# The global queries' values of a banded attention block: ten products on all 128 rows, ahead of the local values, in place of eighteen on 64 rows behind them

## The chip, the cores and the metric

The kernel runs on one core of a Trainium2 chip. The metric is the device time of one execution in microseconds, the median of three runs. The core has a matrix engine (TensorE, "PE" in the profile, its weight loads listed apart as "PEld"), three engines for elementwise work (VectorE "DVE", ScalarE "ACT", GpSimd "POOL") and a queue from which transfers are issued (SyncE, "SP").

## The reference, cut to what matters

```python
B, H, Sl, D, Sg = 8, 8, 512, 64, 32           # batch, heads, local and global tokens
k_all = concat([k_g, k_l]); v_all = concat([v_g, v_l])
out_g = softmax(q_g @ k_all.T / 8) @ v_all     # 32 global queries look at all 544 keys
mask  = abs(i - j) <= 32                       # 512 local queries: 32 global keys, and a band
out_l = softmax([q_l @ k_g.T, band(q_l @ k_l.T)] / 8) @ concat([v_g, v_l])
x = concat([out_g, out_l])                     # 8 x 544 tokens of 512
a, b = x @ w1, x @ w2                          # 512 -> 1024
out = (a * b) @ w3 @ w_out                     # 1024 -> 1024 -> 512
```

All of it is float32. The change touches one term: `softmax(...) @ v_all` of the 32 global queries.

## The kernel before, in words

The program runs over 32 pairs of heads (8 batches, 4 pairs in each). A pair's scores, softmax and values give 544 tokens by 128 columns of `x`; four pairs complete a batch, whose tokens then pass through the two layers of the feed-forward part. The orders in which the engines get their work are written out as a list (`PLAN`), which stays as it is. In the list the feed-forward products of one batch stand between the attention steps of the next, so that TensorE always has something queued.

The product `w3 @ w_out` is folded once at the start, and all weights are unpacked and split in two parts there, by DVE, ACT and POOL, as they arrive; this is the stage up to about 112 us. The feed-forward products are 128 x 128 (`first`: lines L539 to L541; `second`: L571 to L573).

The attention products work on parts of the 128 x 128 array. A product is placed by the 64 rows that its operands lie on and by the columns that its result goes to, so four products of 64 x 64 lie side by side: (x, y) with x the head of the pair (the half of the columns) and y the half of the rows, called lanes in the code. The scores (L377) use eight places of 64 x 32. Each of these float32 products appears in the trace as two load and product instructions.

`values(m)` computes one pair's values, in the PSUM tile `av` of two banks, one for each y:

- L431: the local queries' band, 16 products (4 blocks of 128 keys, 4 lanes). Their moving operand `PT` is assembled by up to eight small copies, by ACT, DVE, POOL or a DMA (`move`, L418 and L420).
- L436: the 32 global queries over the local keys, 16 products of 32 columns. The moving operand `TG[x]` (tile `TGr`) holds their turned probabilities, 128 keys by 4 blocks, and is fetched once per batch and head parity by five DMAs (L510, L511).
- L440: the local queries over the global keys, 8 products.
- L442: the global queries over the global keys, 2 products on the 64 lower rows. Their moving operand `TGg[x]` has 64 partitions, the upper 32 of them zero.

With y = 0 the global queries' result goes to columns 0 to 31 of bank 0, with y = 1 to columns 480 to 511 of bank 1; `values_odd` copies bank 1 out, `values_ends` the first 64 columns of bank 0, `values_sum` adds the rest, and `join_g` (POOL) adds the two partial results of the global queries.

From the sixth pair of scores on, `values_scores` issues the values of one pair and directly behind them the scores of the next.

Of the kernel before, what the change touches and what calls it, by code (L numbers as in the profile page):

```python
# [7 lines left out]
F32 = mybir.dt.float32  # L8
# [210 lines left out]
def band_attention_glu_kernel(  # L219
# [20 lines left out]
    nc = tc.nc  # L240
# [5 lines left out]
    TG = 32 * B  # L246
    S = 544

    const = ctx.enter_context(tc.tile_pool(name="const", bufs=1))
# [18 lines left out]
    TT = const.tile([128, 4, 2, 4, 32], F32, tag="TT", name="TT")  # L268
# [1 line left out]
    PT = const.tile([128, 4, 2, 4, 32], F32, tag="PT", name="PT")  # L270

    VG = [const.tile([128, 2, H, 64], F32, tag="VG0", name="VG0"), None]
    TGg = [const.tile([64, 128], F32, tag=f"TGg{x}", name=f"TGg{x}") for x in range(2)]
    xg = const.tile([128, NP, TG], F32, tag="xg", name="xg")
    sums = p1q.tile([128, 6, 2, 4], F32, tag="sums", name="sums")[:, 0:2]

# [18 lines left out]
    T = {}  # L295
# [59 lines left out]
    def hi_of(dst, src, eng=None):  # L355
        (nc.scalar.copy if eng in (None, nc.scalar) else eng.tensor_copy)(dst, src)  # L356
# [65 lines left out]
    def values(m):  # L422
        b, p = divmod(m, NP)
        av = T["av", m] = ps_1.tile([128, 2, 512], F32, tag="pu", name=f"av{m}", bufs=2)
        V, vg = T["vr", m], VG[b % 2]
        lanes = [(x, y, slice(64 * x, 64 * x + 64), slice(64 * y, 64 * y + 64)) for x in range(2) for y in range(2)]
        go = dict(skip_group_check=True)
        for k in range(4):
            for x, y, c, r in lanes:
                s0, s1 = int(k == y == 0), 4 - int(k == 3 and y)  # L430
                nc.tensor.matmul(av[c, y, 128 * k + 32 * s0 : 128 * k + 32 * s1], V[r, x, k], PT[r, s0:s1, x, k],  # L431
                                 start=(k == 0), stop=False, **go)
        for k in range(4):
            for x, y, c, r in lanes:
                o = 480 * y
                nc.tensor.matmul(av[c, y, o : o + 32], V[r, x, k], T["TG", x][r, p, 32 * k : 32 * k + 32], start=False, stop=False, **go)  # L436
        for a in range(2):
            for x, y, c, r in lanes:
                o = av[c, y].rearrange("p (e c) -> p e c", e=4)[:, :, 32 + 32 * a : 64 + 32 * a]
                nc.tensor.matmul(o, vg[r, a, 2 * p + x], TT[r, 2 - a, x], start=False, stop=bool(a and y), **go)  # L440
        for x in range(2):
            nc.tensor.matmul(av[64 * x : 64 * x + 64, 0, 0:32], vg[0:64, 0, 2 * p + x], TGg[x][:, 32 * p : 32 * p + 32], start=False, stop=True, **go)  # L442

    def values_scores(m):
        values(m - 1)
        scores(m)

    def values_odd(m, eng):
        u = T["u", m] = p2.tile([128, 576], F32, tag="u", name=f"u{m}")
        hi_of(u[:, 64:576], T["av", m][:, 1], eng)  # L450

    def values_ends(m, eng):
        hi_of(T["u", m][:, 0:64], T["av", m][:, 0, 0:64], eng)
# [5 lines left out]
    def join_g(m):  # L459
        b, p = divmod(m, NP)  # L460
        u = T["u", m]
        nc.gpsimd.tensor_add(xg[:, p, 32 * b : 32 * b + 32], u[:, 0:32], u[:, 544:576])  # L462


    def g_scores(b):
# [303 lines left out]
    def head(m):  # L769
# [44 lines left out]
        if me[0] == "av":  # L814
            add(me, only("PE", COST["values"]), t + 4.2, values_need(m), values, m)
            values_read(m)
        take("u", 2, ("u", m), ("cb", m))
        a, d = COST["cb"]
        add(("cb", m), dict(ACT=(a, False, 0), DVE=(d, False, HOLD_H)), t + 4.7, [me], values_odd, m, eng=True)
        a, d = COST["cu"]  # L820
        add(("cu", m), dict(ACT=(a, False, 0), DVE=(d, False, HOLD_H)), t + 4.8, [me, ("cb", m)], values_ends, m, eng=True)
# [4 lines left out]
    def pair(m):  # L826
        b, p = divmod(m, NP)
        t = base(2 * m + 1)
        add(("joing", m), only("POOL", COST["joing"], True), t + 9.0, [("cb", m), ("cu", m)], join_g, m)
        for e in range(2):  # L830
            x = ("x", b, p, e)
            take(f"x{e}", NX[e], x, ("xh", b, p, e))
            add(("xh", b, p, e), only("ACT", COST["xh"]), t + 9.2 + 0.4 * e, [("sum", m)], convert, b, p, e, 0)
            add(("xl", b, p, e), either("xl"), t + 9.6 + 0.4 * e, [("xh", b, p, e)], convert, b, p, e, 1, eng=True)
            read(("xl", b, p, e), x)
            read(("xh", b, p, e), ("u", m))
            read(("xl", b, p, e), ("u", m))
        read(("joing", m), ("u", m))
# [186 lines left out]
    with tc.manual_schedule(engines=None):  # L1025
        idle_products(IDLE[None])
        for _, n, e in list_schedule(steps, after, held):
            fn, args, eng = emit[n]
            k = steps[n][0]
# [65 lines left out]
```

## Time and profile before

| what | value |
|---|---|
| median of three runs | 754.91 us (754.11 to 755.97) |
| the profiled execution: its own time | 755.88 us |
| its span in the profile | 754.1 us |
| TensorE busy | 742.1 us (98%) |
| TensorE weight loads busy | 650.6 us (86%) |
| VectorE, ScalarE, GpSimd busy | 58%, 43%, 11% |

The span is the stretch from the first to the last instruction; the execution's own time has 1.8 us around it. "Busy" means that at least one instruction of the engine was under way, which for a matrix engine that overlaps its instructions says nothing yet on how fast it goes.

### The profile page before, as it was taken

The page shows a single profiled execution, that of the slowest core. Times are in us where ns is not written, and L with a number is a line of the kernel's source. Part 1 is how long each engine was busy: PE and PEld are TensorE (multiplying, and loading weights), DVE is VectorE, ACT ScalarE, POOL GpSimd, SP SyncE. Part 2 cuts the span into 40 slices and gives each one's busy share as a digit, 9 for nine tenths or more (in the row PEclk, how much of TensorE's full clock was granted, in tenths as well). Part 3 has the DMA queues.
Part 4 walks back from the last instruction along what each step waited for, and adds up shares of the span by engine and source line. Part 5 has one row for each costly group of instructions (what it writes and reads, how often), then busy time and mean ns, then how long its engine had stood idle before and what let it go on. Part 6 is the DMA issues. An engine that isn't in the chain of part 4 may idle for free.

```text
span 754.1 us, 22008 instructions
## 1 busy us (share of the span) xinstructions
PE 742.1 (98%) x9232; PEld 650.6 (86%) x9232; DVE 438.8 (58%) x1332; ACT 326.6 (43%) x989; POOL 84.3 (11%) x153
## 2 busy tenths in 40 slices
PE   9999899999999999999999999999999999999998
PEld 5445689989999999889998999899989999999997
DVE  4989997674756455573558465665566464312121
ACT  3649876633544244443435334344454343321111
POOL 4013332232100000000001011000000010000000
PEclk9999999999999999999999999999999999999999
DMA  9878565123422211142112411231113010000000
GB/s 333 269 242 313 176 200 160 47 61 118 132 60 87 99 46 59 52 134 73 31 59 87 128 45 43 90 111 31 60 34 120 16 44 4 32 1 30 1 29 28
DMA packets 46171, 69.47 MB, mean 92 GB/s; under 512 B 7768, under 2 KB 22136, under 8 KB 46072
## 3 DMA queue, kind: packets, MB, share of 16 engines
q1 hardware_dynamic: 46072, 68.07, 28.0%
q8 instruction: 72, 1.18, 0.7%
q14 instruction: 27, 0.22, 0.1%
HBM read 53.74 MB, written 13.37 MB: 89 GB/s over the span
## 4 chain that ended last, share of the span: by engine, by line
PE 81%; DVE 7%; DMA 5%; ACT 3%; issue 1%; SPq 1%; DVEq 0%; ACTq 0%
PE bp L539 8%; PE ap L539 8%; PE acc L573 8%; PE acc L571 8%; PE acc L572 8%; PE ap L540 8%; PE ap L541 8%; PE bp L540 8%; PE bp L541 8%; PE s L377 4%; PE av L431 4%; DMA raw_w<-in_w_t_dram 3%; PE av L440 2%; PE av L436 2%; DMA raw_wo<-in_wo_t_dram 1%
## 5 line engine op out<-in xcount | busy, mean ns | idle before, releaser
L539 PE MATMUL bp<-x,w12h 128*128 128x256 f32 x544 | 153.0, 281 | 0.2 <-DVE g__1210 L549 0.2
L539 PE MATMUL ap<-x,w12h 128*128 128x256 f32 x544 | 152.4, 280 | 0.2 <-ACT x L356 0.2
L540 PE MATMUL ap<-x,w12h 128*128 128x256 f32 x544 | 151.1, 278 | 1.0 <-DVE x L359 1.0
L541 PE MATMUL ap<-x,w12l 128*128 128x256 f32 x544 | 150.8, 277 | 0.0
L540 PE MATMUL bp<-x,w12h 128*128 128x256 f32 x544 | 150.7, 277 | 0.0
L541 PE MATMUL bp<-x,w12l 128*128 128x256 f32 x544 | 150.6, 277 | 0.0
L388 ACT ACTIVATE P<-P,small 128x128 f32<-128x128 f32 x256 | 101.0, 396 | 30.8 <-DVE small L382 30.4
L539 PEld LDWEIGHTS bp<-x,w12h 128*128 128x128 f32 x544 | 102.1, 188 | 5.7 <-issue 3.2
L382 DVE CUSTOM_DVE_ANT_0 P<-s,cs 128x128 f32<-128x128 f32 x256 | 64.2, 284 | 71.7 <-PE s L377 70.0
L539 PEld LDWEIGHTS ap<-x,w12h 128*128 128x128 f32 x544 | 102.2, 188 | 3.6 <-issue 1.4
L540 PEld LDWEIGHTS ap<-x,w12h 128*128 128x128 f32 x544 | 102.4, 188 | 3.0 <-DVE x L359 1.3
L540 PEld LDWEIGHTS bp<-x,w12h 128*128 128x128 f32 x544 | 102.3, 188 | 1.5
L541 PEld LDWEIGHTS ap<-x,w12l 128*128 128x128 f32 x544 | 102.3, 188 | 0.0
L541 PEld LDWEIGHTS bp<-x,w12l 128*128 128x128 f32 x544 | 102.3, 188 | 0.0
L356 ACT COPY u<-av 128x512 f32<-128x512 f32 (+1 forms) x58 | 23.6, 412 | 69.0 <-PE av L442 69.0
L420 ACT COPY PT<-TT 32x256 f32<-32x256 f32 (+1 forms) x99 | 38.6, 390 | 29.9 <-DVE PT L406 14.3
L388 ACT ACTIVATION_READ_ACCUMULATOR P<-P,small 128x1 f32 x256 | 48.0, 188 | 0.0
L684 PE MATMUL w<-wo,w3f 128*128 128x512 f32 x96 | 43.4, 600 | 1.8 <-DVE w3f L597 1.2
L403 DVE STREAM_TRANSPOSE TT<-P 128x1024 f32<-128x1024 f32 x32 | 39.5, 1235 | 0.6
L398 DVE TENSOR_TENSOR P<-P,sums 128x1024 f32<-128x1024 f32 x32 | 39.1, 1222 | 0.6
L431 PEld LDWEIGHTS av<-PT,vr 64*64 64x64 f32 x1024 | 28.1, 132 | 13.0 <-issue 8.4
L462 POOL TENSOR_TENSOR xg<-u 128x32 f32<-128x32 f32 x32 | 8.7, 272 | 267.7 <-ACT u L356 233.4
(771 smaller groups left out, 1340.6 us busy)
## 6 DMA issues: line engine op xcount, KB each, us to landing
raw_w<-in_w_t_dram SPq DMA_DIRECT2D x22, 512.0 KB, 6.1
kq<-in_kp_t_dram SPq DMA_DIRECT2D x32, 272.0 KB, 3.5
out_dram<-o_None SPq DMA_DIRECT2D x33, 256.0 KB, 2.3
qp<-in_q_t_dram SPq DMA_DIRECT2D x32, 256.0 KB, 2.7
vr<-in_v_t_dram SPq DMA_DIRECT2D x32, 256.0 KB, 3.1
gg<-tgs SPq DMA_DIRECT2D x16, 272.0 KB, 2.2
raw_wo<-in_wo_t_dram SPq DMA_DIRECT2D x8, 512.0 KB, 9.3
raw_w3j<-in_w_t_dram SPq DMA_DIRECT2D x8, 512.0 KB, 8.3
```

The source lines that it names most:

```text
L382: nc.vector.tensor_tensor_reduce(Ps[m % 2][:, x, e], T["s", m][:, x, 128 * e : 128 * e + 128], masks[e], -0.125, 3.0e38, ALU.add, ALU.min, ...
L388: nc.scalar.activation(p, p, AF.Exp, bias=T["mn", n][:, e : e + 1], scale=-1.0, accum_out=T["sm", m][:, x, e : e + 1])
L398: eng.tensor_mul(p, p, view(T.pop(("sm", m)), 0, [1, 8], [0, 128]))
L403: nc.vector.transpose(view(TT[:], 0, [32, 8], [256, 4], [1, 32]), view(P, 0, [128, 8], [32, 4], [1, 32]))
L431: nc.tensor.matmul(av[c, y, 128 * k + 32 * s0 : 128 * k + 32 * s1], V[r, x, k], PT[r, s0:s1, x, k], start=(k == 0), stop=False, **go)
L539: nc.tensor.matmul(d, wh[:, k, c, :], x[:, 0, 0:w], start=(k == m % 2 == 0), stop=False, skip_group_check=True)
L540: nc.tensor.matmul(d, wh[:, k, c, :], x[:, 1, 0:w], start=False, stop=False, skip_group_check=True)
L541: nc.tensor.matmul(d, wl[:, k, c, :], x[:, 0, 0:w], start=False, stop=(k == 3), skip_group_check=True)
L571: nc.tensor.matmul(a, gh[:, m % 2, sl], wh[:, c], start=(m == 0), stop=False, **part)
L572: nc.tensor.matmul(a, gh[:, m % 2, sl], wl[:, c], start=False, stop=False, **part)
L573: nc.tensor.matmul(a, gl[:, m % 2, sl], wh[:, c], start=False, stop=(m in (5, 7)), **part)
L684: nc.tensor.matmul(T["w34", t], w3f_of(t, j), wo_of(j), start=(j == 0), stop=(j == 7))
```

## The change

The sixteen products of the global queries over the local keys used half the rows each and were summed in two banks. They become eight that use all 128 rows (one for each block of keys and head), and the two products over the global keys use all 128 rows too: `TGg` grows to 128 partitions, and its rows 32 to 127 are zeroed. The ten stand in front of the local values instead of behind them. Everything goes to bank 0, so `values_odd` copies 480 columns instead of 512, and `join_g` copies where it added. The lines behind the edit have numbers lower by one (L431 becomes L436, L440 becomes L441); the new products are L432.

```diff
-    TGg = [const.tile([64, 128], F32, tag=f"TGg{x}", name=f"TGg{x}") for x in range(2)]
+    TGg = [const.tile([128, 128], F32, tag=f"TGg{x}", name=f"TGg{x}") for x in range(2)]
...
         go = dict(skip_group_check=True)
+
+        for k in range(5):
+            for x in range(2):
+                w, t = (V[:, x, k], T["TG", x][:, p, 32 * k : 32 * k + 32]) if k < 4 else (vg[:, 0, 2 * p + x], TGg[x][:, 32 * p : 32 * p + 32])
+                nc.tensor.matmul(av[64 * x : 64 * x + 64, 0, 0:32], w, t, start=(k == 0), stop=False, **go)
         for k in range(4):
             for x, y, c, r in lanes:
                 s0, s1 = int(k == y == 0), 4 - int(k == 3 and y)
                 nc.tensor.matmul(av[c, y, 128 * k + 32 * s0 : 128 * k + 32 * s1], V[r, x, k], PT[r, s0:s1, x, k],
-                                 start=(k == 0), stop=False, **go)
-        for k in range(4):
-            for x, y, c, r in lanes:
-                o = 480 * y
-                nc.tensor.matmul(av[c, y, o : o + 32], V[r, x, k], T["TG", x][r, p, 32 * k : 32 * k + 32], start=False, stop=False, **go)
+                                 start=(k == 0 and y == 1), stop=False, **go)
         for a in range(2):
             for x, y, c, r in lanes:
                 o = av[c, y].rearrange("p (e c) -> p e c", e=4)[:, :, 32 + 32 * a : 64 + 32 * a]
-                nc.tensor.matmul(o, vg[r, a, 2 * p + x], TT[r, 2 - a, x], start=False, stop=bool(a and y), **go)
-        for x in range(2):
-            nc.tensor.matmul(av[64 * x : 64 * x + 64, 0, 0:32], vg[0:64, 0, 2 * p + x], TGg[x][:, 32 * p : 32 * p + 32], start=False, stop=True, **go)
+                nc.tensor.matmul(o, vg[r, a, 2 * p + x], TT[r, 2 - a, x], start=False, stop=bool(a), **go)
...
-        hi_of(u[:, 64:576], T["av", m][:, 1], eng)
+        hi_of(u[:, 64:544], T["av", m][:, 1, 0:480], eng)
...
-        nc.gpsimd.tensor_add(xg[:, p, 32 * b : 32 * b + 32], u[:, 0:32], u[:, 544:576])
+        nc.gpsimd.tensor_copy(xg[:, p, 32 * b : 32 * b + 32], u[:, 0:32])
```

What stands on TensorE at one pair (the fifteenth), before, from the last feed-forward product to the first global queries' products. A row gives line, result, operands and the result's shape; "x10" are ten such in a row, and in brackets stand the engines and DMA queues that a row waits for.

```order
L573 MATMUL acc_1_128_4222<-w34h_483,gl__4180 128x512
L431 MATMUL av_4233<-PT,vr_3760 64x96 [waits DMAHW4_49,Pool_49]
L431 MATMUL av_4233<-PT,vr_3760 64x128 [waits DMAHW1_49]
L431 MATMUL av_4233<-PT,vr_3760 64x96
L431 MATMUL av_4233<-PT,vr_3760 64x128 x10
L431 MATMUL av_4233<-PT,vr_3760 64x96
L431 MATMUL av_4233<-PT,vr_3760 64x128
L431 MATMUL av_4233<-PT,vr_3760 64x96
L436 MATMUL av_4233<-TGr_3428,vr_3760 64x32 x2
L436 MATMUL av_4233<-TGr_3470,vr_3760 64x32 x2
```

The same place of the changed program.

```order
L572 MATMUL acc_1_128_4110<-w34h_483,gl__4068 128x512
L432 MATMUL av_4121<-TGr_3332,vr_3656 64x32 [waits DMAHW4_49]
L432 MATMUL av_4121<-TGr_3374,vr_3656 64x32
L432 MATMUL av_4121<-TGr_3332,vr_3656 64x32
L432 MATMUL av_4121<-TGr_3374,vr_3656 64x32
...
L432 MATMUL av_4121<-TGg_98,VG_1139 64x32
L432 MATMUL av_4121<-TGg_99,VG_1139 64x32
L436 MATMUL av_4121<-PT,vr_3656 64x96 [waits Pool_49]
L436 MATMUL av_4121<-PT,vr_3656 64x128 [waits DMAHW1_49]
```

The ten products come first, one head after the other, and the waits for `PT`'s copies (Pool, and the second DMA queue) moved behind them; one wait for a DMA queue stays on the first. Before, the end of the same pair's values, up to the next pair's scores:

```order
L436 MATMUL av_4233<-TGr_3470,vr_3760 64x32 x2
L440 MATMUL av_4233<-TT,VG_1171 64x4x32 x8
L442 MATMUL av_4233<-TGg_98,VG_1171 64x32
L442 MATMUL av_4233<-TGg_99,VG_1171 64x32
L377 MATMUL s_4276<-KT_92,qp_3513 32x128 x32
```

And in the changed program:

```order
L436 MATMUL av_4121<-PT,vr_3656 64x96
L441 MATMUL av_4121<-TT,VG_1139 64x4x32 x8
L377 MATMUL s_4156<-KT_92,qp_3417 32x128 x32
```

The products on 64 rows are now one block, and the scores stand directly behind the local queries' products over the global keys. On the other engines the order is unchanged.

## Rows read from the trace of the kernel before

**Rows 1.** The profile's page: span, TensorE's busy time, granted clock in 40 slices.

```profile
span 754.1 us, 22008 instructions
PE 742.1 (98%) x9232; PEld 650.6 (86%) x9232; DVE 438.8 (58%) x1332; ACT 326.6 (43%) x989; POOL 84.3 (11%) x153
...
PEclk9999999999999999999999999999999999999999
```

**Rows 2.** Stages, busy us (instructions) per engine: PE, PEld, DVE, ACT, POOL.

```profile
45.00:115.00 70.00, 65.16 (x930) 45.57 (x932) 64.38 (x161) 53.49 (x143) 21.52 (x24) 1.00 0.68 228
115.00:650.00 535.00, 534.18 (x7342) 489.34 (x7324) 320.44 (x1039) 229.77 (x749) 52.69 (x95) 1.00 0.23 72
```

**Rows 3.** The same stages, PE and PEld, instructions of L442 alone.

```profile
45.00:115.00 70.00, 1.55 (x20) 1.53 (x20) 1.00 0.68 228
115.00:650.00 535.00, 7.09 (x108) 6.95 (x108) 1.00 0.23 72
```

**Rows 4.** Timeline of TensorE's products around the fifteenth pair: start, us until the last's end.

```profile
304.92 0.39 PE L572 MATMUL acc<-w34l,gh__4174 128*128 128x512 f32 x1
305.15 0.40 PE L573 MATMUL acc<-w34h,gl__4180 128*128 128x512 f32 x1
305.48 1.05 PE L431 MATMUL av<-PT,vr 64*64 64x96 f32 x32
306.35 0.62 PE L436 MATMUL av<-TGr,vr 64*64 64x32 f32 x32
306.79 0.65 PE L440 MATMUL av<-TT,VG 64*64 64x128 f32 x16
307.25 0.26 PE L442 MATMUL av<-TGg,VG 64*64 64x32 f32 x4
307.44 1.16 PE L377 MATMUL s<-KT,qp 64*32 64x128 f32 x64
308.53 0.39 PE L539 MATMUL bp<-x,w12h 128*128 128x256 f32 x1
308.75 0.28 PE L540 MATMUL bp<-x,w12h 128*128 128x256 f32 x1
```

**Rows 5.** Timeline of its weight loads in the same stretch.

```profile
304.93 0.19 PEld L573 LDWEIGHTS acc<-w34h,gl__4180 128*128 128x128 f32 x1
305.48 0.86 PEld L431 LDWEIGHTS av<-PT,vr 64*64 64x64 f32 x32 [0.36 <-issue]
306.24 0.61 PEld L436 LDWEIGHTS av<-TGr,vr 64*64 64x64 f32 x32
307.44 0.89 PEld L377 LDWEIGHTS s<-KT,qp 64*32 64x32 f32 x64
308.76 0.19 PEld L541 LDWEIGHTS bp<-x,w12l 128*128 128x128 f32 x1
```

**Rows 6.** Products by tile and line: ns of one, minimum/median/maximum; first and last start.

```profile
L431 PE MATMUL av<-PT,vr x1024: 242/269/321, 47.4 to 648.3; 64*64 64x128 f32 x116, 64*64 64x96 f32 x55
L436 PE MATMUL av<-TGr,vr x1024: 189/219/219, 48.3 to 648.8; 64*64 64x32 f32 x171
L440 PE MATMUL av<-TT,VG x512: 269/269/299, 48.7 to 649.2; 64*64 64x128 f32 x171
L442 PE MATMUL av<-TGg,VG x128: 189/204/219, 49.2 to 649.3; 64*64 64x32 f32 x128
...
L377 PE MATMUL s<-KT,qp x2048: 266/269/294, 9.0 to 633.7; 64*32 64x128 f32 x187
```

**Rows 7.** Weight loads of the sixteenth pair, in brackets the idle time before.

```profile
319.71 0.40 PEld L431 LDWEIGHTS av<-PT,vr 64*64 64x64 f32 x8 [0.36 <-issue]
320.47 0.64 PEld L431 LDWEIGHTS av<-PT,vr 64*64 64x64 f32 x24 [0.36 <-DMA PT<-TT]
```

**Rows 8.** Products around the fifth pair.

```profile
111.02 0.28 PE L541 MATMUL ap<-x,w12l 128*128 128x256 f32 x1
112.11 1.11 PE L431 MATMUL av<-PT,vr 64*64 64x96 f32 x30 [0.82 <-ACT PT L420]
```

**Rows 9.** Fetches of `TGg`, 100 to 115 us: issues, and their time to landing.

```profile
L511 SPq DMA_DIRECT2D TGg<-gg x2: 430/430/430, 105.2 to 108.8; - x2
...
DMA to landing us min/median/max: 3.1/3.1/3.1
```

## The prediction, made before the changed kernel ran

> **What bounds the kernel now.** I read the page's head first: TensorE is busy for 742.1 of 754.1 us, every other engine for 58% or less, and its granted clock stands at full speed (2.4 GHz) in all 40 slices [rows 1]. A busy matrix engine need not be a full one, so the stages come next. From 115 to 650 us TensorE is busy for 534.18 of 535 us [rows 2]: 0.8 us of idle time in all, while DVE has 320 us and ACT 230. Here nothing waits but the others, and whatever a pair of heads adds to TensorE's row moves the end by as much. From 45 to 115 us TensorE is busy 65.16 of 70 us and DVE 64.38 [rows 2]; it idles for unpacked weights there, and a small addition can vanish in that. The two products of L442, four instructions a pair, count the pairs: 20 instructions, five pairs, in the early stage, and 108, twenty-seven pairs, in the steady one [rows 3].
>
> So the question is what one pair's values take on TensorE, and the timeline of one pair answers it [rows 4]. From the first load of L431 at 305.48 to the scores at 307.44 it takes 1.96 us: L431 0.87, L436 0.44, L440 0.46, L442 0.19. The reader should see that these are differences of starts; the lengths behind the starts overlap.
>
> **What sets the pace inside.** L436 has 32 instructions (two to a float32 product) on four places that work side by side: eight rounds. From the first start to the last end is 0.62 us, one instruction is recorded with 0.219 [rows 4, 6], so 0.40 us for seven rounds: 57 ns a round. Streaming 32 columns cannot need that: a 128-column instruction takes 80 ns longer than the shortest 32-column one (269 against 189 ns, [rows 6]), 0.83 ns a column, which makes 27 ns for 32. What takes 57 is the weight load. The first product after a change of shape shows its length, since it must wait for a load that nothing hides: L431's longest is 52 ns over its median (321 against 269), with 64 columns of weights; L377's is 25 over (294 against 269), with 32; L539's first is 110 over the product behind it (0.39 against 0.28 us), with 128 [rows 4, 6]. The load goes by the columns of one place, 0.8 to 0.9 ns each, with one place at work (L539), four (L431) or eight (L377) alike. L442 runs on two places only, and its longest is the same 219 ns as L436's [rows 6]: fewer neighbours did not make its second load faster.
>
> **What the change does to a pair.** Removed: L436, eight rounds, and L442, two rounds on half the places. Added: twenty instructions on two places (128 rows, 64 columns each), that is ten rounds. The instructions fall from 36 to 20, the rounds stay at ten. That is the heart of my forecast: rows were not the limit, loads in a row at one place were, and there are as many as before.
>
> *Saved.* L436: 0.44 us, and 0.03 more since L440's first round (longest 299 against a median of 269, [rows 6]) no longer waits for a load behind L436's. L442: not the 0.19 between its start and L377's. A change of shape starts when the last product is nearly out of the array: L442's last ends at 307.51 and L377's load stands at 307.44, 0.07 earlier [rows 4, 5]. Without L442, L440's block ends at 306.79 + 0.65 = 307.44, so L377 may start at 307.37 instead of 307.44. That is 0.07 to 0.08. Together 0.55 us.
>
> *Added.* Ten rounds of 57 ns: 0.57 us. No row shows a place of 128 rows by 64 columns; the bounds are 30 ns a round (27 of streaming and a little issue, if the load were hidden) and 114 (if the two places had to load in turn). I take 57, since two places gave it in L442. Then a new change of shape, 128 rows to 64, ahead of L431. The one in front of the pair stays. Its price in the row: L573 to L431's load is 0.33 us where two L57x products in a row are 0.23 apart (304.92 and 305.15), so 0.10 us with nothing streaming [rows 4], and then a first load of 0.05 us that nothing hides. Sum 0.15; the bounds are 0, if this kind of change needs no emptying, and 0.20 as from L377 to L539: L377's block ends at 308.60, so its last product (0.269) started at 308.33 and streamed 128 columns to 308.44; L539 stands at 308.53, 0.09 later, and its load takes 0.11. I take 0.15, the change of the same place in the program: "[0.36 <-issue]" in front of L431's loads [rows 5] is that gap, and the loads, which otherwise run ahead, do not cross it. In the Trainium skill, "TensorEngine Tiling (Array Packing)", section "Key Properties", a change of tiling mode drains the engine; that speaks against this change. By it the pair pays the 0.15; without it, 0. The trace agrees for the changes that it holds, but none of them keeps the column places and alters the rows alone, as the new one does.
>
> *Net of one pair:* 0.57 + 0.15 - 0.55 = +0.17 us.
>
> *What moves with it.* The waits for `PT`'s copies now stand behind 0.7 us of work. That helps where TensorE waited for them: the sixteenth pair loses 0.56 us in mid-block for a DMA into `PT` [rows 7]; with L431 starting 0.72 later, at 320.43, the copy that arrived at 320.47 is there, so the pair gains about 0.55 - 0.17 = 0.4. The fifth pair stands idle from 111.3 to 112.11 for a copy [rows 8], but its `TGg` was issued at 108.85 and lands 3.1 us later, at 111.95 [rows 9], and is now wanted early: gain and loss cancel, 0. The other 26 steady pairs show 1.96 us without a wait. The first four lie in the stage where TensorE idles 4.8 us for weights; I count them 0, with -0.8 (one wait of the fifth's size, 0.82, hidden) to +0.7 (four times 0.17, nothing absorbed) as bounds. ACT's copy is 32 columns shorter, POOL copies instead of adding, the zeroed tile has more partitions and no more columns: all beside TensorE, which is released by none of them in the steady stage, so 0; if the cover were gone, a copy of `u` would be worth some tens of ns a pair, in the change's favour.
>
> *Sum.* 26 x 0.17 - 0.4 = +4.0 us. The profiled execution took 755.88 us by its own count (span 754.1 and 1.8 around it), so 759.9 on that; the median of the runs is 1.0 lower, 754.91, and what is predicted is a median: **758.9 us**, 0.5% slower.
>
> **The rivals.**
> *The load is hidden and the pair gets faster.* If 57 ns comes from the number of instructions at work rather than from the load, half as many run at the streaming pace of 30 ns: 0.30 + 0.15 - 0.55 = -0.10 a pair, -3.0 in all, 751.9 us. It decides from 40 ns a round downwards. Against it stands L442's 219 ns on two places, and the loads' equal price for one, four and eight. Chance 0.07.
> *No emptying for rows alone.* The column places stay the same, so L431's loads might run ahead as L440's do. Then 0.57 - 0.55 = +0.02 a pair, and with the hidden waits 0 in all: 755 us, no change. For it: no row shows this change of shape. Against it: every change of shape that there is pays. Chance 0.14.
> *The two heads take turns.* The new products alternate head by head and share all rows. If the second instruction of one product had to leave before the other head's first, each of five steps costs a further slot of some 15 ns: +0.07 a pair, +5.8 in all, 760.7 us. Chance 0.08. If the places could not load side by side at all, ten rounds cost 1.14: +0.74, 774 us. Chance 0.03.
> *Loads wait for products on the same rows.* By this a round is 57 + 30 = 87 ns: 0.87 + 0.15 - 0.55 = +0.47 a pair, 26 of them less 0.4: +11.8, 766.7 us. Against it: L541's load starts at 308.76, 0.01 after L540's product started on the same 128 rows [rows 4, 5]. Chance 0.04. This is what the Trainium skill states in "TensorE: Matmul & The Clock Gate", "Part 3: Packing small matmuls" (loads overlap products in flight only on other row groups); the trace disagrees where the whole array is used.
>
> **How the numbers follow.** The forecast has the remaining 0.64; its own range, with the switch at 0.12 to 0.18, a round at 55 to 59 ns and the first four pairs' bounds, is 757 to 761. The range that leaves out no more than 2 in 10 reaches down to the case without emptying and up to the heads in turn: **754.5 to 761.5 us**, 0.86 by the chances, less where I mistook a price. About 0.3%, 2.3 us, is what a measurement here can tell from no change. Slower by more: the forecast (nearly all of it), the turns and both costly cases, 0.76. Within: the case without emptying and a tail of the forecast, 0.16. Faster: the hidden load, 0.08 with a tail.
>
> **What would show it.** In the changed profile the ten products' block should take 0.57 us from its first start to the last and its loads some 57 ns apart at one place; L436 (the local band) should start 0.72 us after the block, behind an idle gap of its own, with its longest products again 52 ns over the median; L441 should follow without its first round's stall, and the scores' first load stand 0.07 us before the end of L441's last product. From the last feed-forward product to the scores a pair should be 0.17 longer. Rounds at 30 ns, or a band whose loads run ahead into the new block, make me wrong; so does a steady stage with idle time on TensorE, which would mean that some wait moved in front of the ten products.

## The result, and the profile after

| | before | after |
|---|---|---|
| median of four runs, taken side by side | 755.2 us (754.11 to 755.97) | 759.3 us (758.74 to 760.38) |
| ratio after/before | | 1.0057, 95% interval 1.0039 to 1.0075 |
| the profiled execution: its own time, span | 755.88 us, 754.1 us | 758.86 us, 757.0 us |

The changed kernel is slower by 0.6%. The forecast was 758.9 us. The page's head answers [rows 1]:

```profile
span 757.0 us, 20984 instructions
PE 746.4 (99%) x8720; PEld 649.6 (86%) x8720; DVE 439.6 (58%) x1332; ACT 325.3 (43%) x989; POOL 83.1 (11%) x153
```

TensorE has 512 product instructions fewer (256 products) and is busy for 4.3 us longer. The other engines hardly moved. Where the time went is seen in one pair. The timeline of products around the fifteenth pair answers [rows 4]; the second fence is the timeline of its weight loads [rows 5].

```profile
306.39 0.40 PE L572 MATMUL acc<-w34h,gl__4068 128*128 128x512 f32 x1
306.72 0.66 PE L432 MATMUL av<-TGr,vr 128*64 128x32 f32 x16
307.20 0.29 PE L432 MATMUL av<-TGg,VG 128*64 128x32 f32 x4
307.42 1.05 PE L436 MATMUL av<-PT,vr 64*64 64x96 f32 x32
308.29 0.62 PE L441 MATMUL av<-TT,VG 64*64 64x128 f32 x16
308.84 1.16 PE L377 MATMUL s<-KT,qp 64*32 64x128 f32 x64
```

```profile
306.72 0.55 PEld L432 LDWEIGHTS av<-TGr,vr 128*64 128x64 f32 x16 [0.36 <-issue]
307.18 0.20 PEld L432 LDWEIGHTS av<-TGg,VG 128*64 128x64 f32 x4
307.42 0.86 PEld L436 LDWEIGHTS av<-PT,vr 64*64 64x64 f32 x32
308.19 0.48 PEld L441 LDWEIGHTS av<-TT,VG 64*64 64x64 f32 x16
308.84 0.89 PEld L377 LDWEIGHTS s<-KT,qp 64*32 64x32 f32 x64 [0.17 <-issue]
```

From the first product to the scores the pair takes 306.72 to 308.84, 2.12 us, where it took 1.96. The ten products, up to the band, are 0.70 of it (forecast 0.72). What is left, from the band to the scores, is 1.42; it was 1.96 with L436 and L442 in it, so leaving these two out saved 0.54 (forecast 0.55). The loads show the two kinds of seam. From L436 to L441, one shape, the first load stands 0.10 us ahead of its product (308.19 and 308.29); but L436's first load, 307.42, stands at the same place as its first product. It did not run ahead across the change from 128 rows to 64; it stands 0.07 us before the end of the last L432 product (307.20 + 0.29 = 307.49), as the scores' first load before the change stood 0.07 us before the end of L442 [rows 4].

The lengths of single products answer [rows 6] (ns, minimum/median/maximum):

```profile
L436 PE MATMUL av<-PT,vr x1024: 242/269/320, 49.4 to 651.8; 64*64 64x128 f32 x117, 64*64 64x96 f32 x54
L432 PE MATMUL av<-TGr,vr x512: 222/223/243, 48.7 to 650.7; 128*64 128x32 f32 x171
L441 PE MATMUL av<-TT,VG x512: 269/269/269, 50.3 to 652.2; 64*64 64x128 f32 x171
```

The band's longest product is still 51 ns over its median: its first load is not hidden. L441's longest is equal to its median: the stall of L440's first round (299 ns) is gone, as forecast.

The sixteenth pair, which had waited for a DMA [rows 7], answers with these loads:

```profile
321.11 0.55 PEld L432 LDWEIGHTS av<-TGr,vr 128*64 128x64 f32 x16 [0.36 <-PE acc L571]
...
321.81 0.86 PEld L436 LDWEIGHTS av<-PT,vr 64*64 64x64 f32 x32
```

Its scores stand at 323.23: 2.12 us, like every other pair; before, they stood at 322.27, 2.56 us after 319.71. So this pair gained 0.44.

The first five pairs did not go as the forecast had them. The fifth had waited for a copy and started at 112.11 [rows 8]; now it starts at 110.83, 1.28 us earlier, and waits neither for `PT` nor for `TGg`. Then its scores' loads stop for 1.15 us, with no wait shown, and that takes the gain back:

```profile
110.83 0.55 PEld L432 LDWEIGHTS av<-TGr,vr 128*64 128x64 f32 x16
...
112.95 0.86 PEld L377 LDWEIGHTS s<-KT,qp 64*32 64x32 f32 x60 [0.17 <-issue]
114.96 0.14 PEld L377 LDWEIGHTS s<-KT,qp 64*32 64x32 f32 x4 [1.15 <-issue]
```

The sixth pair starts at 127.83, before at 127.80. In the ten profiled executions of this document the fifth pair starts anywhere from 109.87 to 113.64, so two of them do not tell what the early stage does with an addition.

The forecast left one wait out. Behind the sixteenth pair TensorE waits once in the whole steady stage for DVE, for the low part `gl` of the feed-forward's inner product. The chain of waits from 328 to 340 us, first before, then after:

```profile
PE acc L573 <- DVE gl__4688 L359: 0.7, 1, 0.7
```

```profile
PE acc L572 <- DVE gl__4560 L359: 0.4, 1, 0.4
```

The later TensorE arrives there, the less it waits: 0.3 us came back. In the profiled executions the sum is thus +4.0 for the 26 steady pairs (25 of them took 0.157 or 0.158 us more, the tenth 0.106; the rows round to 0.16), less 0.44, less 0.3: +3.3, and measured are 758.86 - 755.88 = +3.0. The rest stands in feed-forward products that the change does not touch. Before, from 199 to 206 us and from 339 to 349 us, those of 256 columns followed each other at 0.118 us; in the same places of the changed program they do at 0.113. Ten such steps take 1.18 us before (344.89 to 346.07) and 1.14 after (345.39 to 346.53), with a granted clock of 1.00 in both; the two stretches give 0.2 and 0.3 us, a little more than the rest, and steps of some 0.01 us between other pairs go the other way. Why the pace differs is not shown. The medians differ by 4.1, and their interval (2.9 to 5.7 us) holds both sums.

### The profile page after: what moved, and what is told of

The parts are those of the page before. It is cut to its first block, busy times and chain, and to the rows that moved or that the text cites. A ratio compares the mean times of both kernels' runs of the same rounds, so it can differ in the third digit from the quotient of the medians.

```text
span 757.0 us, 20984 instructions
## 1 busy us (share of the span) xinstructions
PE 746.4 (99%) x8720; PEld 649.6 (86%) x8720; DVE 439.6 (58%) x1332; ACT 325.3 (43%) x989; POOL 83.1 (11%) x153
## 4 chain that ended last, share of the span: by engine, by line
PE 88%; DVE 6%; ACT 3%; issue 2%; DMA 1%; SPq 0%; DVEq 0%; ACTq 0%
PE bp L538 8%; PE acc L572 8%; PE ap L538 8%; PE acc L570 8%; PE acc L571 8%; PE ap L539 8%; PE bp L540 8%; PE bp L539 8%; PE ap L540 8%; PE s L377 4%; PE av L436 3%; PE w L683 3%; PE av L432 3%; PE av L441 2%; ACT P L388 1%
## 5 line engine op out<-in xcount | busy, mean ns | idle before, releaser
L356 ACT COPY u<-av 128x480 f32<-128x480 f32 (+1 forms) x58 | 22.7, 397 | 73.7 <-PE av L441 73.7
L683 PEld LDWEIGHTS w<-wo,w3f 128*128 128x128 f32 x96 | 17.6, 189 | 24.8 <-issue 18.0
L377 PE MATMUL s<-KT,qp 64*32 64x128 f32 x2048 | 37.1, 274 | 0.9 <-issue 0.9
```

The costliest lines, as they stand in the source:

```text
L377: nc.tensor.matmul(st[32 * a : 32 * a + 32, x, 128 * e : 128 * e + 128], q[r, 128 * e + 32 * a : 128 * e + 32 * a + 32], k[r, o : o + 128] ...
L683: nc.tensor.matmul(T["w34", t], w3f_of(t, j), wo_of(j), start=(j == 0), stop=(j == 7))
```

## The experiments

Theory: (a) a round of weight loads of 64 columns at one place takes 57 ns, whatever the rows and however many places; so ten rounds for ten save nothing; (b) the new change of shape costs about 0.15 us a pair and is the whole loss. Rivals: the place in front of the band costs; the streaming or the number of instructions sets the round; the wide rows themselves are slow. In the diffs "-" is the kernel named as the base. Every measured time stands against the kernel before, run beside it.

**The place alone.** Base: the kernel before. The sixteen 64-row products move in front of the band, nothing else.

```diff
         for k in range(4):
             for x, y, c, r in lanes:
+                o = 480 * y
+                nc.tensor.matmul(av[c, y, o : o + 32], V[r, x, k], T["TG", x][r, p, 32 * k : 32 * k + 32], start=(k == 0), stop=False, **go)
+        for k in range(4):
+            for x, y, c, r in lanes:
                 s0, s1 = int(k == y == 0), 4 - int(k == 3 and y)
                 nc.tensor.matmul(av[c, y, 128 * k + 32 * s0 : 128 * k + 32 * s1], V[r, x, k], PT[r, s0:s1, x, k],
-                                 start=(k == 0), stop=False, **go)
-        for k in range(4):
-            for x, y, c, r in lanes:
-                o = 480 * y
-                nc.tensor.matmul(av[c, y, o : o + 32], V[r, x, k], T["TG", x][r, p, 32 * k : 32 * k + 32], start=False, stop=False, **go)
+                                 start=False, stop=False, **go)
```

> The kernel before with one edit: L436's sixteen products of 64 x 64 stand in front of the local values; L442's two stay at the end. Theory 1 (a pair pays 58 ns a round of 64-column weight loads and 0.15 us for the extra change of shape): no extra change of shape, rounds as before, so a steady pair takes 1.96 to 2.00 us from its first product to the scores, and the waits for PT hide as they do in the changed kernel: 753.5 to 755, that is 4 to 6 us under the changed kernel. Rival (the place in front is what costs, whatever the shape): the pair takes 2.12 us and the time is about 759.

Measured: 755.98 us against 755.02; ratio 1.001 (0.9996 to 1.0024). Its timeline of products, fifteenth pair:

```profile
306.70 0.67 PE L431 MATMUL av<-TGr,vr 64*64 64x32 f32 x32
307.19 1.03 PE L435 MATMUL av<-PT,vr 64*64 64x96 f32 x32
...
308.48 0.26 PE L442 MATMUL av<-TGg,VG 64*64 64x32 f32 x4
308.67 1.16 PE L377 MATMUL s<-KT,qp 64*32 64x128 f32 x64
```

306.70 to 308.67 is 1.97: the place costs a pair nothing. The gain that I expected from the hidden wait is in the trace (the sixteenth pair takes 320.94 to 323.02, 2.08) and not in the median. In this execution the sixth pair began at 128.88, where before it was 127.80: from 92.12 to 95.32 us the feed-forward products follow each other at 0.21 to 0.22 us instead of 0.11 to 0.12, since the clock had fallen. The windows of 2.5 us (TensorE's busy time and its granted clock), of this kernel and then of before:

```profile
90.00:92.50 2.50, 1.48 (x8) 0.91 0.93 341
92.50:95.00 2.50, 2.50 (x14) 0.50 0.11 42
```

```profile
90.00:92.50 2.50, 1.91 (x16) 1.00 0.86 320
92.50:95.00 2.50, 2.50 (x24) 1.00 0.08 29
```

A granted clock of 0.50 is the lower level, 1.2 GHz. Before has the same wait in front (0.96 us, ending at 90.59, here at 91.41) and keeps 2.4 GHz. The lower clock is not the whole reason why the median missed my 753.5 to 755: three of the twelve runs had a mean granted clock of 1.0, and they took 755.4 to 756.3. What kept them there is open.

**The shape change alone.** Base: the kernel before. Only L442's two products get 128 rows; they stay at the end, the rounds stay ten, and there is one more change of shape.

```diff
-    TGg = [const.tile([64, 128], F32, tag=f"TGg{x}", name=f"TGg{x}") for x in range(2)]
+    TGg = [const.tile([128, 128], F32, tag=f"TGg{x}", name=f"TGg{x}") for x in range(2)]
...
-            nc.tensor.matmul(av[64 * x : 64 * x + 64, 0, 0:32], vg[0:64, 0, 2 * p + x], TGg[x][:, 32 * p : 32 * p + 32], start=False, stop=True, **go)
+            nc.tensor.matmul(av[64 * x : 64 * x + 64, 0, 0:32], vg[:, 0, 2 * p + x], TGg[x][:, 32 * p : 32 * p + 32], start=False, stop=True, **go)
```

> The kernel before with L442's two products alone on all 128 rows (the rows above zero in the moving operand): same products, same rounds, same place, one more change of shape in each pair (64 rows to 128, then to the scores' 64 x 32). Theory 1 (the price is the change of shape): L442's first load stands some 0.1 us after L440's last streaming ends, and the pair takes 2.12 to 2.15 us in place of 1.965; by the time, 27 pairs of 0.17 less what the wait for DVE's gl at 333 us gives back (up to 0.9): 757.5 to 759.5. Rival (rows alone change without emptying, and the changed kernel loses by its rounds): the pair stays at 1.96 to 2.0, the time within 1 us of before.

Measured: 759.34 us against 754.05; ratio 1.0073 (1.0055 to 1.009). Its timeline, fifteenth pair:

```profile
305.17 1.05 PE L431 MATMUL av<-PT,vr 64*64 64x96 f32 x32
...
306.47 0.65 PE L440 MATMUL av<-TT,VG 64*64 64x128 f32 x16
307.05 0.31 PE L442 MATMUL av<-TGg,VG 128*64 128x32 f32 x4
307.29 1.16 PE L377 MATMUL s<-KT,qp 64*32 64x128 f32 x64
```

The pair takes 2.12 us, as in the changed kernel. L440 to L442 grew from 0.46 [rows 4] to 0.58, and L442 to the scores from 0.19 to 0.24: 0.17 from the rounded rows. The column places and the rounds are those of before, so the change of rows alone reproduces the whole loss of the change. (A product on 128 rows is recorded with 222 ns or more, the shortest on 64 rows with 189 [rows 6]; that it leaves the array later may be part of the price and was not tried apart.)

**The ten at the end.** Base: the changed kernel. The loop of L432 moves behind L441's, so the shapes change as often, and the band comes first again.

```diff
-        for k in range(5):
-            for x in range(2):
-                w, t = (V[:, x, k], T["TG", x][:, p, 32 * k : 32 * k + 32]) if k < 4 else (vg[:, 0, 2 * p + x], TGg[x][:, 32 * p : 32 * p + 32])
-                nc.tensor.matmul(av[64 * x : 64 * x + 64, 0, 0:32], w, t, start=(k == 0), stop=False, **go)
...
-                nc.tensor.matmul(o, vg[r, a, 2 * p + x], TT[r, 2 - a, x], start=False, stop=bool(a), **go)
+                nc.tensor.matmul(o, vg[r, a, 2 * p + x], TT[r, 2 - a, x], start=False, stop=bool(a and y), **go)
+        for k in range(5):
+            for x in range(2):
+                w, t = (V[:, x, k], T["TG", x][:, p, 32 * k : 32 * k + 32]) if k < 4 else (vg[:, 0, 2 * p + x], TGg[x][:, 32 * p : 32 * p + 32])
+                nc.tensor.matmul(av[64 * x : 64 * x + 64, 0, 0:32], w, t, start=False, stop=(k == 4), **go)
```

> The changed kernel with its ten products of 128 rows moved behind the local queries' products, to the end of the pair's values. Theory 1: the changes of shape are as many, so a steady pair takes 2.12 us again (2.08 to 2.16), and the waits for PT's copies come back, 0.4 to 1.2 us in all: 759.5 to 760.8. Rival (the place in front is what costs): back to about 755.

Measured: 758.39 us against 755.02; ratio 1.006 (1.0048 to 1.0073). The fifteenth pair, 308.01 (band) to 310.13 (scores), is 2.12 again. In the profiled execution, which took 760.11, the sixteenth waits for its DMA once more (2.71), but then TensorE does not wait for `gl` at all between 328 and 340 us: what one wait costs, the next gives back. The other four runs took 758.2 to 759.5, so the median ends under my 759.5 to 760.8 and is no longer than the changed kernel's 759.3; the hidden waits that the place in front should give were not seen in the time. Which wait was shorter in those runs is not shown.

**Half the weight columns.** Base: the changed kernel. Each of the ten is cut into two of 32 weight columns: the same rows, shape changes and result, double the products.

```diff
-                nc.tensor.matmul(av[64 * x : 64 * x + 64, 0, 0:32], w, t, start=(k == 0), stop=False, **go)
+                for h in (0, 32):
+                    nc.tensor.matmul(av[64 * x + h : 64 * x + h + 32, 0, 0:32], w[:, h : h + 32], t, start=(k == 0), stop=False, **go)
```

> The changed kernel with each of the ten products cut in two of 32 weight columns: twenty products, 40 instructions a pair, on four places of 128 x 32; the result is complete. Theory 1 (the round goes by the weight columns of one place): 32 columns load in about 27 ns, the round falls from 58 to 30 to 35 ns, the block from 0.55 to about 0.32 us, the pair from 2.12 to about 1.88, the time to 751.5 to 754. Rival (the block goes by the number of instructions, some 14 ns each as in L436): 40 instructions take 0.56 us, the pair stays at 2.12 to 2.15, the time at 759 to 760.

Measured: 757.47 us against 755.02; ratio 1.0031 (1.0013 to 1.0049). Its timeline, fifteenth pair:

```profile
306.24 0.46 PE L433 MATMUL av<-TGr,vr 128*32 128x32 f32 x32
...
306.73 1.05 PE L437 MATMUL av<-PT,vr 64*64 64x96 f32 x32
...
308.15 1.16 PE L377 MATMUL s<-KT,qp 64*32 64x128 f32 x64
```

Forty instructions take less than twenty did: 0.49 us to the band instead of 0.70, and the pair takes 1.91. Its weight loads give the round:

```profile
306.23 0.35 PEld L433 LDWEIGHTS av<-TGr,vr 128*32 128x32 f32 x32 [0.36 <-issue]
306.48 0.20 PEld L433 LDWEIGHTS av<-TGg,VG 128*32 128x32 f32 x8
```

The 32 loads over `TGr` take 0.35 us. The last of them is 0.11 long, and the four places start 0.007 one behind the other; what remains is seven rounds of 31 ns (expected 30 to 35). In the changed kernel 16 loads of 64 columns take 0.55, the last is 0.14 long and there are two places: seven rounds of 58 ns. The eight loads over `TGg` are out of step: they start over 0.10 us, where rounds of 31 ns would need 0.05. Why is not shown. The run also doubles the places, from two to four; but L436 before, on four places with 64 columns, had the long round too, so it is the columns. The rival by which instructions set the pace (2.12 or more) falls. But the time missed my 751.5 to 754. Three places of the profiled execution took it back. In the early stage TensorE ran at the lower clock once, and the sixth pair began at 128.49 instead of 127.80. The wait for `gl` grew from 0.7 to 1.9 us. And the clock fell behind that wait; the timeline of products there, and two windows:

```profile
335.69 0.55 PE L573 MATMUL acc<-w34h,gl__4720 128*128 128x512 f32 x1 [1.89 <-DVE gl__4720 L359]
336.04 0.63 PE L571 MATMUL acc<-w34h,gh__4718 128*128 128x512 f32 x1
...
338.81 0.41 PE L540 MATMUL bp<-x,w12h 128*128 128x256 f32 x1
339.03 0.41 PE L541 MATMUL bp<-x,w12l 128*128 128x256 f32 x1
...
339.45 0.28 PE L540 MATMUL ap<-x,w12h 128*128 128x256 f32 x1
339.56 0.28 PE L541 MATMUL ap<-x,w12l 128*128 128x256 f32 x1
```

```profile
336.50:340.00 3.50, 3.50 (x17) 3.28 (x16) 0.90 (x4) 1.07 (x4) 0.00 (x0) 0.58 0.05 14
340.00:345.00 5.00, 5.00 (x41) 4.79 (x40) 1.98 (x3) 1.64 (x3) 0.62 (x1) 1.00 0.28 105
```

Products that stand 0.11 us apart at 339.45 stand 0.22 apart at 338.81, with a granted clock of 0.58 in the window. Twelve steps from 336.04 to 339.24 take 3.2 us; at the full pace (three of 0.228 and nine of 0.113) they take 1.7. So the lower clock cost 1.5 us. Its three runs with a mean granted clock of 1.0 took 753.6 to 755.5, the seven below 755.9 to 759.3.

**Four of ten.** Base: the changed kernel. The global queries' products with three of the four blocks of keys are left out.

```diff
-        for k in range(5):
+        for k in (0, 4):
```

> The changed kernel with four of the ten products (the first and the last block of keys; three blocks of the global queries' values are left out). Theory 1: four rounds for ten, 6 x 58 ns = 0.35 us less a pair, the block's last product to the band's first load unchanged at 0.15 us, the pair 1.77, the time 749 to 751. Rival (the new shape has a large fixed cost and the rounds are cheap, 30 ns): 0.18 less a pair, the pair 1.94, the time 754 to 755.

Measured: 751.93 us against 755.02; ratio 0.9958 (0.9943 to 0.9974). Its timeline, fifteenth pair:

```profile
304.77 0.31 PE L432 MATMUL av<-TGr,vr 128*64 128x32 f32 x4
...
305.12 1.05 PE L436 MATMUL av<-PT,vr 64*64 64x96 f32 x32
...
306.54 1.16 PE L377 MATMUL s<-KT,qp 64*32 64x128 f32 x64
```

It takes 0.35 us to the band, where ten products took 0.70. Six rounds are 0.35 us, 58 ns each, and what is left of the ten's 0.70 is 0.12 for the seam: the two terms of my sum, now measured apart. The pair takes 1.77, as expected. The time is about 1 us over my 749 to 751: the wait for `gl` grew to 1.8 us, and the sixth pair began at 129.05, again with the lower clock ahead of it (granted 0.58 from 60 to 62.5 us, behind a wait of 2.25 us for the weights). Its three runs with a mean granted clock of 0.999 or 1.0 took 747.6 to 749.8, the seven below 751.6 to 753.8.

**Twice the moving columns.** Base: the changed kernel. The ten products stream 64 columns; 32 result columns of the local queries are spoilt by it.

```diff
-                w, t = (V[:, x, k], T["TG", x][:, p, 32 * k : 32 * k + 32]) if k < 4 else (vg[:, 0, 2 * p + x], TGg[x][:, 32 * p : 32 * p + 32])
-                nc.tensor.matmul(av[64 * x : 64 * x + 64, 0, 0:32], w, t, start=(k == 0), stop=False, **go)
+                w, t = (V[:, x, k], T["TG", x][:, p, 32 * min(k, 2) : 32 * min(k, 2) + 64]) if k < 4 else (vg[:, 0, 2 * p + x], TGg[x][:, 32 * min(p, 2) : 32 * min(p, 2) + 64])
+                nc.tensor.matmul(av[64 * x : 64 * x + 64, 0, 0:64], w, t, start=(k == 0), stop=False, **go)
```

> The changed kernel with 64 moving columns in the ten products in place of 32 (the 32 more are a neighbour's, so columns 32 to 63 of the result are spoilt); weights as they were. Theory 1 (a round is one load of 64 weight columns, the streaming lies under it): 64 columns stream in 53 ns, still under the load, the round stays at 58 to 60 ns, the block at 0.55 us, the pair at 2.12 to 2.16. Rival (load and streaming follow each other at a place, 28 and 30 ns): the round grows to 85 ns, the block to 0.8 us, the pair to 2.38.

One run, 760.38 us. Its weight loads, fifteenth pair:

```profile
307.70 0.55 PEld L432 LDWEIGHTS av<-TGr,vr 128*64 128x64 f32 x16 [0.36 <-issue]
308.17 0.20 PEld L432 LDWEIGHTS av<-TGg,VG 128*64 128x64 f32 x4
308.44 0.86 PEld L436 LDWEIGHTS av<-PT,vr 64*64 64x64 f32 x32
```

Both groups of L432's loads take as long as in the changed kernel, 0.55 and 0.20: the round stays at 58 ns. To the band it is 0.73 (0.70 there), and the 0.03 more stands behind the last loads (308.17 to 308.44, there 307.18 to 307.42), where the last product streams 32 columns more, 27 ns by the prediction's 0.83 ns a column. The pair takes 2.15, as expected. Streaming does not set the pace.

**Fewer rounds without a new shape.** Can the rounds fall and the shape stay? In the kernel before, each band block at the rim has an unused 32-column slot of `PT`. GpSimd copies one block of `TG` into it (29 of the 32 pairs), the band's product there grows from 96 to 128 columns, and L436 leaves out that block: one round a lane fewer. The first version has the order of before, the second that of "the place alone".

```diff
+                        nc.gpsimd.tensor_copy(PT[r, 3 * y, x, 3 * y], T["TG", x][r, p, 96 * y : 96 * y + 32])
...
-                s0, s1 = int(k == y == 0), 4 - int(k == 3 and y)
+                s0, s1 = (0, 4) if T["in", m] else (int(k == y == 0), 4 - int(k == 3 and y))
...
+                if T["in", m] and k == 3 * y:
+                    continue
```

> The kernel before, with two of the eight rounds of L436 taken away without a change of shape: the band's first and last product of a lane leave 32 of their 128 columns unused just where the global queries' result goes, so GpSimd copies one block of the global queries' probabilities into that slot of PT (four copies of 64 x 32 a pair), and four of the sixteen products fall away; done for the 29 pairs whose probabilities are there in time. Theory 1: six rounds for eight, 0.117 us less a pair, the pair 1.85, some 3 us less in all, of which the wait for DVE's gl at 333 us gives back up to 1: 752 to 754. Rival (GpSimd's copies, about 1.1 us a pair, come too late and TensorE waits for them, or what they push back): no faster than before, 755 or more.

Measured: 761.76 us against 754.41; ratio 1.01 (1.0075 to 1.0126). The expectation was wrong. Its timeline:

```profile
311.90 1.10 PE L438 MATMUL av<-PT,vr 64*64 64x128 f32 x32
312.82 0.50 PE L445 MATMUL av<-TGr,vr 64*64 64x32 f32 x23
...
313.85 1.16 PE L377 MATMUL s<-KT,qp 64*32 64x128 f32 x64
```

The pair takes 1.95, where I expected 1.85. The two rounds less do save 0.12 (from `TGr`'s products to L449's 0.32 us instead of 0.44), but the band's block is 0.92 instead of 0.87, as its products at the rim now stream more, and L451 takes 0.24 to the scores where it took 0.19 before, for a reason that was not traced. In its execution the loads of one pair's scores stop for 2.54 us with nothing shown that they wait for, at 200.5 us, and behind the stop the granted clock is 0.67 from 203 to 205.5 us and 0.64 from 205.5 to 208:

```profile
199.71 0.80 PEld L377 LDWEIGHTS s<-KT,qp 64*32 64x32 f32 x53
203.05 0.17 PEld L377 LDWEIGHTS s<-KT,qp 64*32 64x32 f32 x11 [2.54 <-issue]
```

From this pair to the next the execution loses 4.3 us on the kernel before, stop and lower clock together; by the last pair it has lost 6.8. One of the six runs had a mean granted clock of 1.0 and took 760.86, so the lower clock is not the whole loss. Whether GpSimd's copies cause it, as the rival has it, is not shown.

> The same with the global queries' products (twelve in 29 pairs, all of 64 x 64) in front of the local values. Theory 1: the pair 1.85 as well, the waits for PT hidden behind 0.35 us; 751.5 to 754.5. Rival: as for the last, 755 or more.

Measured: 755.97 us against 754.41; ratio 1.0024 (1.0007 to 1.0042). In its timeline the pair runs from 305.76 (`TG`'s products) to 307.68 (scores), 1.92 (expected 1.85), so 0.05 less than before, 1.3 us in 26 pairs. In the profiled execution (755.07) the sixteenth pair takes most of it back: it waits 1.3 us for the DMA into `PT` and takes 3.48, where it took 2.56 before. The time missed my 751.5 to 754.5. Neither version beats the kernel before.

## Why the prediction was right

- **Rounds, not rows or instructions.** Right. L432's ten rounds take 58 ns each (forecast 57), measured by leaving out six and read from the loads. Of the three things that could set the pace, only the weight columns do: halving them gave 31 ns, doubling the streaming left 58, doubling the instructions did not lengthen the block. The rival with a hidden load (30 ns) and the one with heads in turn both fall with this number.
- **The change of shape.** Right in place, a little too dear: 0.12 at the band's seam, where I took 0.15. With the columns as before and only the rows altered, the loads stop all the same until the last product is nearly out. The run with only L442 on 128 rows shows it without the rest of the change: pair 2.12. The Trainium skill, "TensorEngine Tiling (Array Packing)", section "Key Properties", says that a change of tiling mode drains the engine; these runs agree for a change of rows alone.
- **Loads on the same rows.** The rival of 87 ns a round fell. The rule of the Trainium skill, "TensorE: Matmul & The Clock Gate", "Part 3: Packing small matmuls" (loads overlap products only on other row groups), does not hold here: both heads use all rows, and a round takes 58 ns, about the load alone, also with 64 columns streaming.
- **The net of a pair.** Right: +0.157 for a forecast +0.17.
- **The hidden waits.** Right for the sixteenth pair (-0.44, forecast -0.4). For the first five pairs the forecast's 0 came out by luck: at the fifth pair's start they were 1.28 us ahead, some 0.8 of it that pair's wait, and a stop in its scores, which the sum does not have, gave it back. The forecast let gain and loss cancel at the fifth pair, because `TGg` would land too late; it landed in time (issued at 107.35, 3.2 us to landing), and the wait was gone without a price.
- **A missing term.** The wait for `gl` at 334 us is one of the 0.8 idle us that I named and did not follow. It gave back 0.3 us here, and in two of the experiments it took 1.1 to 1.2 us of their gains. With this wait, the stop and the pace of the feed-forward products outside the sum, the median's closeness (759.3 for 758.9) is better than the terms earned.

## What to carry to other kernels

Count the work of small products in rounds: weight columns loaded one behind the other at one place. Where the moving columns stream in no more time than the load takes, as the 32 and 64 columns here, filling all the rows with half as many instructions buys nothing while that number stays. Count the changes of shape beside them: here one change of rows alone cost as much as nearly three rounds (0.157 us for 58 ns). And follow a saving to the next wait behind it: a stage that got shorter arrived earlier at DVE's `gl` and handed 1.1 to 1.2 us of its gain back there.

## What was not expected of the hardware

- Short waits can cost more than their length. Behind idle times of 1 to 2.5 us TensorE's granted clock fell to its lower level in the profiled executions of five of the experiments (the place alone, half the weight columns, four of ten, twice the moving columns, and the first version with fewer rounds), and the feed-forward's 256-column products that ran at it stood 0.21 to 0.22 us apart instead of 0.11 to 0.12, for about 3 us. Four of these kernels kept a mean granted clock of 1.0 in other runs. The wait of 0.96 us near 90 us stands in all ten profiled executions, and the clock fell behind it in two. What decides it is not shown.
- A round with 32 weight columns takes 31 ns and one with 64 takes 58: the 32 columns more cost 27 ns, within the 0.8 to 0.9 ns a column that the prediction read from the first loads, and some 4 ns of each round do not go by the columns. What these are was not tried.
- The same 256-column products follow each other at 0.113 us in most stretches and at 0.118 in some, with a granted clock of 1.00; which stretches differs between executions. The cause stays open.
- Weight loads can stop in the middle of one pair's scores with no wait shown: 1.15 us in the changed kernel, 2.54 us with GpSimd's extra copies. The trace has a transfer of the queue for instructions close to both (16 KB, from 112.51 to 113.38 us with the stop ending at 114.96, and from 200.66 to 201.60 with the stop ending at 203.05). Whether the loads waited for it was not tried, and the cause stays open.
